# Attention scores as plain float32 products in the two row halves of the array, in place of split q and k

## The chip, the cores and the metric

The kernel runs on one core of one Trainium2 chip. What counts is the device time of one execution in microseconds (us), the median of three runs. In the rows, PE is TensorE, PEld its weight loads, DVE VectorE, ACT ScalarE, POOL GpSimd and SP SyncE, which issues most of the DMAs.

## The reference

Three stages follow each other: banded attention, a dense layer pair with x - tanh(x), and a second pair with a softmax-weighted, normalised middle. All arrays are float32.

```python
scores = scale * np.matmul(q, k.transpose(0, 1, 3, 2))        # B=4, H=8, S=576, D=64
scores = np.where(masks[None], scores, -1e9)                   # heads 0-3: the last 32 keys;
attn = softmax(scores)                                         # heads 4-7: every 4th of the last 128
x = np.matmul(attn, v)                                         # -> 2304 tokens x 512
h = x @ w_in                                                   # 512 -> 2048
y = (h - np.tanh(h)) @ w_out                                   # 2048 -> 512
h = y @ w_in2                                                  # 512 -> 1024
solu = h * softmax(h)
ln = (solu - mean(solu)) / np.sqrt(var(solu) + 1e-6) * g_ln
out = ln @ w_out2                                              # 1024 -> 512
```

## The kernel before, in words

The 2304 tokens are six groups of 384. The attention of a group is eight **units**; there are 48. A unit has two heads (h) and two blocks of 96 queries (b), each block with 128 keys, so four score tiles of 96 x 128. A unit goes through these pieces:

- its q and k are loaded (`load_qk`) as one tile `qkr`, with the 64 numbers of a head along the rows; its v is loaded by `load_v`;
- scores: units 0 to 19 (`NFU = 20`) in `qk_f32`, four plain float32 products on rows 0 to 63, into one PSUM bank. Units 20 to 47 in two halves (`qk_half`): `prep_unit` has rounded q and k to the short float32 format (`float32r`) and taken the remainder, the rows 64 to 127 hold a second copy of the data, and one product with 128 rows and 256 columns per score tile gives both parts of the sum; VectorE adds them and the mask;
- the four mask-and-minimum instructions on VectorE (L204 or L231), four exponentials on ScalarE (`sm_exp`), the division on GpSimd (`sm_norm`);
- the four transposes of the probabilities (`tr_pe`, tile `tp`), copied by ScalarE to `pt` (L260);
- `pv_pe`, for two units at a time: the eight products with v, whose outputs lie in rows 0 to 63 for one head and 64 to 127 for the other; ScalarE and VectorE take them out of PSUM (L284, L286).

The first eight units are computed at the start, with VectorE and ScalarE also decoding and splitting the first weights (L98 to L134). After that the dense layers run: `mm1(s)` is twelve products of 128 x 128 by 384 (L348) and `mm2(s)` the same (L375). The work of the other 40 units is threaded in between by hand. **A slot is one mm1 or one mm2**; slot 2s has mm1(s), slot 2s+1 has mm2(s-5). `plan` gives each piece its slot: the scores of unit u stand in slot p, its transposes and pv in later ones.

```python
p = 4 * u - 41 if u >= 2 * NU else (2, 6, 8, 12, 14, 16, 18, 20)[u - u0]
q = p + 2 if u >= 2 * NU or u < u0 + 4 else p + 1
...
if u0 <= u - 1 < u1:
    piece(q, lambda u=u: tr_pe(u - 1, a_ps, "at"))
if u % 4 == 1 and u0 <= u - 5 < u1:
    for w in (u - 5, u - 3):
        piece(q + 1, lambda w=w: pv_pe(w, a_ps, "at"))
```

The TensorE part of a piece comes behind the slot's mm1 or mm2. What takes it out of PSUM is queued on ScalarE or VectorE only in the next slot, behind that slot's weight decoding and tanh. All pieces take their PSUM banks in turn from one pool of two, `a_ps`; in the start-up they come from `st_ps`, with two banks each for scores, transposes and pv. Each engine works its instructions in the order written.

Of the kernel before, what the change touches and what calls it, by code (L numbers as in the profile page):

```python
# [7 lines left out]
F32 = mybir.dt.float32  # L8
# [16 lines left out]
NQ, NK = 96, 128  # L25
NU = 8
QC, KC = 4 * NQ, 4 * NK
KD = DM // 128
NF = FF // 128
NF2 = FF2 // 128  # L30
# [10 lines left out]
def tile_kernel(ctx: ExitStack, tc: tile.TileContext, qk, vw, cst, w_in, w_out, w_in2, w_out2, g_ln, out):  # L41
# [4 lines left out]
    wi_p = ctx.enter_context(tc.tile_pool(name="wi", bufs=1, side="left"))  # L46
    wo_p = tc.alloc_tile_pool(name="wo", bufs=1, side="left")
    cv_p = tc.alloc_tile_pool(name="cv", bufs=2, side="left")
    ys_p = qs_p = None
    g_p = ctx.enter_context(tc.tile_pool(name="g", bufs=2, side="right"))  # L50
    x_p = ctx.enter_context(tc.tile_pool(name="x", bufs=2, side="right"))
    at_p = tc.alloc_tile_pool(name="at", bufs=2, side="right")
# [8 lines left out]
    def mask_of(u, j):  # L61

        g, r = divmod(u, NU)
        hp, bp = divmod(r, 2)
        if hp < 2:
            return 0 if (4 * g + 2 * bp + j) % 6 == 0 else 1
        return (0, 2, 1)[g % 3]
# [80 lines left out]


    xt, un = {}, {}  # L150
    NFU = 20

    def load_qk(u):

        if u < NU:
            r = wo_p.tile([128, 1024], F32, tag=f"wo{NU + u}", name=f"qkr{u}")[:, 0:QC + KC]
        else:
            r = at_p.tile([128, QC + KC], F32, tag="qkr", name=f"qkr{u}")
        n = 64 if u < NFU else 128
        nc.sync.dma_start(out=r[:n], in_=qk[u, :n])  # L160
        un[u] = dict(r=r)

    def load_v(u):
# [6 lines left out]
            load_qk(u)  # L170
            load_v(u)

    def prep_unit(u):
        if not NFU <= u < NU * NG:
            return []
        r = un[u]["r"]
        s = qs_p.tile([128, QC + 2 * KC], F32R, tag="qks", name=f"qks{u}")
        un[u]["s"] = s
        return [
            lambda: nc.scalar.copy(out=s[:, 0:QC + KC], in_=r),  # L180
            lambda: nc.vector.tensor_tensor(out=s[64:128, 0:QC], in0=r[64:128, 0:QC],
                                            in1=s[64:128, 0:QC].bitcast(F32), op=ALU.subtract),
            lambda: nc.vector.tensor_tensor(out=s[:, QC + KC:], in0=r[:, QC:],
                                            in1=s[:, QC:QC + KC].bitcast(F32), op=ALU.subtract),
        ]

    def new_p(u):
        d = un[u]
        d["p"] = at_p.tile([NQ, 4, NK], F32, tag="p", name=f"p{u}", bufs=3)
        for t in ("nm", "sm", "rs"):  # L190
            d[t] = at_p.tile([NQ, 4], F32, tag=t, name=f"{t}{u}")

    def qk_f32(u, pool, tag):

        d = un[u]
        new_p(u)
        ps = pool.tile([128, 512], F32, tag=tag, name=f"qkp{u}")[:NQ, 0:KC].rearrange("p (b k) -> p b k", b=4)
        for b in range(4):
            nc.tensor.matmul(ps[:, b], d["r"][:64, b * NQ:(b + 1) * NQ],  # L199
                             d["r"][:64, QC + b * NK:QC + (b + 1) * NK], start=True, stop=True)  # L200

        def then():
            for b in range(4):
                nc.vector.tensor_tensor_reduce(  # L204
                    out=d["p"][:, b], in0=ps[:, b], in1=masks[:, mask_of(u, b % 2)], op0=ALU.add, op1=ALU.min,
                    scale=-0.125, scalar=3.0e38, accum_out=d["nm"][:, b:b + 1])
        return then

    def qk_half(u, hf, pool, tag):

        d = un[u]
        if hf == 0:
            new_p(u)
        ps = pool.tile([128, 512], F32, tag=tag, name=f"qkp{u}_{hf}")[:NQ, 0:4 * NK].rearrange(
            "p (b c k) -> p b c k", b=2, c=2)
        s = d["s"]
        for j in range(2):
            b = 2 * hf + j
            nc.tensor.matmul(  # L219
                ps[:, j], s[:, b * NQ:(b + 1) * NQ],  # L220
                s[:, QC:].rearrange("p (c k) -> p c k", c=2)[:, :, b * NK:(b + 1) * NK],
                start=True, stop=True)

        def then():
            m0, m1 = mask_of(u, 0), mask_of(u, 1)
            m = masks[:, 0:2] if m0 != m1 else masks[:, m0:m0 + 1].to_broadcast([NQ, 2, NK])
            p2 = d["p"][:, 2 * hf:2 * hf + 2]
            nc.vector.tensor_tensor(out=p2, in0=ps[:, :, 0], in1=m, op=ALU.add)
            for j in range(2):
                b = 2 * hf + j  # L230
                nc.vector.tensor_tensor_reduce(  # L231
                    out=d["p"][:, b], in0=ps[:, j, 1], in1=d["p"][:, b], op0=ALU.add, op1=ALU.min,
                    scale=-0.125, scalar=3.0e38, accum_out=d["nm"][:, b:b + 1])
        return then

    def sm_exp(u, bs=range(4)):
        d = un[u]
        for b in bs:
            nc.scalar.activation(out=d["p"][:, b], in_=d["p"][:, b], func=AF.Exp, scale=-1.0,  # L239
                                 bias=d["nm"][:, b:b + 1], accum_out=d["sm"][:, b:b + 1])  # L240

# [46 lines left out]


    st_ps = tc.alloc_tile_pool(name="st_ps", bufs=2, space=PSUM, side="left")  # L290
    load_qk(0)
    w_load()
    nc.sync.dma_start(out=cst_sb, in_=cst)
# [5 lines left out]
            w_load()  # L299
    back = None  # L300
    for r in range(NU + 3):
        t = qk_f32(r, st_ps, "qk") if r < NU else None
        b1 = pv_pe(r - 4, st_ps, "pv") if r % 2 == 0 and 0 <= r - 4 < NU else None
        b2 = tr_pe(r - 2, st_ps, "tr") if 0 <= r - 2 < NU else None
        if t:
            t()
        if back:
            back("h")
        if t:
            sm_exp(r)  # L310
        if 0 <= r - 1 < NU:
            sm_norm(r - 1)
        if back:
            back("l")
        back = b1
        if b2:
            b2()
        if r in SW:
            w_step(dve=True)
        if r in (4, 5):  # L320
            load_v(r + 2)
        if r in (6, 8):
            load_unit(NU + r // 2 - 3)
    back()
    nc.sync.dma_start(out=gl_sb, in_=g_ln)
    st_ps.release()

# [8 lines left out]
    def at(slot, fn):  # L338
        later.setdefault(slot, []).append(fn)
# [44 lines left out]
            nc.scalar.dma_start(out=y_dr[:, :, g * G:(g + 1) * G], in_=ys)  # L384

    u0, u1 = NU, NU * NG
    preps = []

    def piece(slot, fn):
        todo.setdefault(slot, []).append(fn)  # L390

    def plan():


        ready = 0
        for u in range(u0, u1 + 2):
            p = 4 * u - 41 if u >= 2 * NU else (2, 6, 8, 12, 14, 16, 18, 20)[u - u0]
            q = p + 2 if u >= 2 * NU or u < u0 + 4 else p + 1
            if u < u1:
                at(p + 1, lambda u=u: preps.extend(prep_unit(u + 1)))  # L400
                for i in (1, 1, 2):
                    at(p + i, lambda: preps.pop(0)() if preps else None)
                if u < NFU:
                    piece(p, lambda u=u: qk_f32(u, a_ps, "at"))
                    at(p + 1, lambda u=u: sm_exp(u))
                    at(p + 2, lambda u=u: sm_norm(u))
                else:
                    piece(p, lambda u=u: qk_half(u, 0, a_ps, "at"))
                    at(p + 2, lambda u=u: sm_exp(u, (0, 1)))
                    piece(p + 1, lambda u=u: qk_half(u, 1, a_ps, "at"))  # L410
                    at(p + 3, lambda u=u: sm_exp(u, (2, 3)))
                    at(p + 4, lambda u=u: sm_norm(u))
                at(p + 1, lambda u=u: load_unit(u + 2))
            if u0 <= u - 1 < u1:
                piece(q, lambda u=u: tr_pe(u - 1, a_ps, "at"))
# [3 lines that stand above are left out]
# [31 lines left out]
    for s in range(NS + LAG):  # L450
        if s == NS - NF:
            assert not todo and not later and not (wq or wld or wa or wf or wh), (todo, later)
            a_ps.release()
            at_p.release()
            qs_p.release()
            cv_p = tc.alloc_tile_pool(name="cv2", bufs=2, side="left", reuse_waits="tile")
            new_tops()
            h2a = tc.alloc_tile_pool(name="h2a", bufs=1, space=PSUM, side="right", reuse_waits="tile")
            p2 = tc.alloc_tile_pool(name="p2", bufs=2, side="right", reuse_waits="tile")
            wq.extend(wq2)  # L460
            w_load()
            w_load()
        for half in range(2):
            if ys_p is None and not (wq or wld or wa or wf or wh):
                cv_p.release()
                ys_p = tc.alloc_tile_pool(name="ys", bufs=1, side="left", reuse_waits="tile")
                qs_p = tc.alloc_tile_pool(name="qs", bufs=2, side="left", reuse_waits="tile")
            if half == 0:
                cur = mm1(s) if s < NS else None
            elif s >= LAG:  # L470
# [151 lines left out]
def _layout(q, k, v, moe_w_in, moe_w_out, moe2_w_in, moe2_w_out, moe2_g_ln):  # L622
    import numpy as np

    def blocks(a, n, back):
# [7 lines left out]
        for g in range(NG):  # L633
            for r in range(NU):
                hp, bp = divmod(r, 2)
                for h in range(2):
                    for b in range(2):
# [3 lines left out]
                        else:  # L641
# [3 lines left out]
        return o.reshape(NG * NU, 2, 2, n, D)  # L645

    qb, kb, vb = blocks(q, NQ, 0), blocks(k, NK, WIN), blocks(v, NK, WIN)
    qkt = np.concatenate([qb.transpose(0, 4, 1, 2, 3).reshape(NG * NU, D, QC),
                          kb.transpose(0, 4, 1, 2, 3).reshape(NG * NU, D, KC)], axis=2)
    qkt = np.concatenate([qkt, qkt], axis=1)  # L650
    vt = vb.transpose(0, 3, 2, 1, 4).reshape(NG * NU, NK, 4 * D)

    def bits(w):
# [38 lines left out]
```

## Time and profile before

| | us |
|---|---|
| median of three runs (727.55 to 729.39) | 728.31 |
| span of the profiled execution | 726.3 |
| TensorE busy in it | 708.8 |
| VectorE busy | 440.5 |
| ScalarE busy | 386.9 |
| GpSimd busy | 114.4 |

Of the profiled execution only the span is given, with no device time of its own; it is 2.0 us below the median of the runs. Busy times are sums of instructions, and TensorE's are pipelined, so that a busy TensorE still leaves open how fast it goes. The stages lie in time as follows: units 0 to 7 until about 37 us, mm1 and mm2 with units 8 to 19 until about 134 us, with units 20 to 47 until about 404 us, then the rest of the dense layers.

### The profile page before, as it was taken

The page shows a single profiled execution, that of the slowest core. Times are in us where ns is not written, and L with a number is a line of the kernel's source. Part 1 is how long each engine was busy: PE and PEld are TensorE (multiplying, and loading weights), DVE is VectorE, ACT ScalarE, POOL GpSimd, SP SyncE. Part 2 cuts the span into 40 slices and gives each one's busy share as a digit, 9 for nine tenths or more (in the row PEclk, how much of TensorE's full clock was granted, in tenths as well). Part 3 has the DMA queues.
Part 4 walks back from the last instruction along what each step waited for, and adds up shares of the span by engine and source line. Part 5 has one row for each costly group of instructions (what it writes and reads, how often), then busy time and mean ns, then how long its engine had stood idle before and what let it go on. Part 6 is the DMA issues. An engine that isn't in the chain of part 4 may idle for free.

```text
span 726.3 us, 11583 instructions
## 1 busy us (share of the span) xinstructions
PE 708.8 (98%) x4160; PEld 650.7 (90%) x4160; DVE 440.5 (61%) x1169; ACT 386.9 (53%) x1010; POOL 114.4 (16%) x190
## 2 busy tenths in 40 slices
PE   6888999999999999999999999999999999999997
PEld 5678999999999999999999999999888888888885
DVE  5987676476676667766666435554555454555452
ACT  5778776465555555555555334543354444444444
POOL 2212311011010111111110100101133221323110
PEclk9999999999999999999999999999999999999999
DMA  9985621132223211322230015543001110110001
GB/s 274 341 263 177 189 78 55 65 110 66 66 66 109 66 60 44 107 66 66 66 109 1 1 49 170 175 142 132 1 15 59 44 58 16 59 44 30 15 29 44
DMA packets 30313, 64.05 MB, mean 88 GB/s; under 512 B 2992, under 2 KB 16816, under 8 KB 30256
## 3 DMA queue, kind: packets, MB, share of 16 engines
q1 hardware_dynamic: 27088, 58.59, 25.4%
q10 hardware_dynamic: 3168, 4.72, 1.8%
q8 instruction: 33, 0.54, 0.3%
q14 instruction: 24, 0.20, 0.1%
HBM read 53.86 MB, written 9.44 MB: 87 GB/s over the span
## 4 chain that ended last, share of the span: by engine, by line
PE 92%; DVE 4%; DMA 1%; issue 1%; ACT 1%; POOL 0%; SPq 0%; ACTq 0%; POOLq 0%
PE y L375 28%; PE h L348 26%; PE po L585 14%; PE h L523 14%; PE zt L566 2%; PE pv L275 2%; PE tp L254 2%; PE qkp L219 2%; PE qkp L199 2%; DMA qkr<-in_qk_dram 1%; DVE p L204 1%; DVE wy_wi L123 1%; DVE wi L98 1%; DVE wi L134 0%; POOL p L247 0%
## 5 line engine op out<-in xcount | busy, mean ns | idle before, releaser
L348 PE MATMUL h<-x,wi 128*128 128x384 f32 x1152 | 220.0, 340 | 1.6 <-DVE t L359 1.6
L375 PE MATMUL y<-gs,wo 128*128 128x384 f32 x1152 | 217.4, 339 | 0.0
L375 PEld LDWEIGHTS y<-gs,wo 128*128 128x128 f32 x1152 | 199.8, 189 | 1.8
L348 PEld LDWEIGHTS h<-x,wi 128*128 128x128 f32 x1152 | 197.4, 189 | 3.2 <-DVE t L359 2.1
L247 POOL TENSOR_TENSOR p<-p,rs 96x512 f32<-96x512 f32 x47 | 57.2, 1217 | 350.4 <-DVE rs L245 323.5
L365 DVE TENSOR_TENSOR gs<-t,gs 128x384 fp32r<-128x384 f32 x96 | 77.4, 806 | 52.7 <-ACT gs L362 52.6
L523 PE MATMUL h<-w2i,yt 128*128 128x512 f32 x432 | 104.9, 397 | 0.0
L585 PE MATMUL po<-w2o,z 128*128 128x512 f32 x432 | 104.1, 396 | 0.1
L574 ACT ACTIVATE z<-zt,gl_sb 128x128 fp32r<-128x128 f32 x144 | 50.9, 366 | 96.6 <-PE zt L566 48.5
L585 PEld LDWEIGHTS po<-w2o,z 128*128 128x128 f32 x432 | 80.7, 188 | 20.4 <-ACT z L574 1.9
L523 PEld LDWEIGHTS h<-w2i,yt 128*128 128x128 f32 x432 | 79.7, 187 | 18.4
L359 DVE TENSOR_TENSOR t<-h,t 128x384 f32<-128x384 f32 x96 | 53.0, 552 | 69.8 <-ACT t L356 69.7
L575 DVE SCALAR_TENSOR_TENSOR z<-zt,gl_sb,z 128x128 fp32r<-128x128 f32 x144 | 48.9, 350 | 68.9 <-ACT z L574 68.9
L356 ACT ACTIVATE t<-h 128x384 f32<-128x384 f32 x96 | 46.8, 487 | 79.4 <-PE h L348 76.4
L239 ACT ACTIVATE p<-p,nm 96x128 f32<-96x128 f32 x192 | 74.9, 392 | 21.4 <-DVE nm L204 20.8
L362 ACT CAST gs<-t 128x384 fp32r<-128x384 f32 x96 | 48.8, 508 | 46.8 <-DVE t L359 46.8
L540 DVE SCALAR_TENSOR_TENSOR u<-h,e 128x1024 f32<-128x1024 f32 x18 | 22.0, 1224 | 24.1 <-ACT e L539 24.1
L199 PE MATMUL qkp<-qkr 64*96 64x128 f32 x160 | 29.4, 339 | 7.3 <-DMA qkr<-in_qk_dram 5.4
L441 POOL TENSOR_TENSOR yt<-yr,yt 128x1024 fp32r<-128x1024 f32 x9 | 22.8, 2538 | 86.8 <-DVE yt L440 86.8
L239 ACT ACTIVATION_READ_ACCUMULATOR p<-p,nm 96x1 f32 x192 | 36.1, 188 | 0.0
L199 PEld LDWEIGHTS qkp<-qkr 64*96 64x96 f32 x160 | 24.1, 205 | 11.8 <-DMA qkr<-in_qk_dram 5.7
L286 DVE TENSOR_TENSOR x<-pv,x 128x384 fp32r<-128x384 f32 x24 | 16.3, 699 | 25.1 <-ACT x L284 24.6
(64 smaller groups left out, 657.6 us busy)
## 6 DMA issues: line engine op xcount, KB each, us to landing
qkr<-in_qk_dram SPq DMA_DIRECT2D x28, 448.0 KB, 3.4
raw_wi<-in_w_in_dram SPq DMA_DIRECT2D x16, 511.8 KB, 7.2
raw_wo<-in_w_out_dram SPq DMA_DIRECT2D x16, 511.8 KB, 6.7
v<-in_vw_dram SPq DMA_DIRECT2D x48, 128.0 KB, 3.3
y_dr<-ys ACTq DMA_DIRECT2D x6, 768.0 KB, 3.9
yr<-y_dr SPq DMA_DIRECT2D x9, 512.0 KB, 4.2
out_dram<-o SPq DMA_DIRECT2D x18, 256.0 KB, 2.0
qkr<-in_qk_dram SPq DMA_DIRECT2D x20, 224.0 KB, 4.8
```

Source lines behind the costliest of these rows:

```text
L199: nc.tensor.matmul(ps[:, b], d["r"][:64, b * NQ:(b + 1) * NQ], d["r"][:64, QC + b * NK:QC + (b + 1) * NK], start=True, stop=True)
L239: nc.scalar.activation(out=d["p"][:, b], in_=d["p"][:, b], func=AF.Exp, scale=-1.0, bias=d["nm"][:, b:b + 1], accum_out=d["sm"][:, b:b + 1])
L247: eng.tensor_tensor(out=d["p"], in0=d["p"], in1=d["rs"].unsqueeze(2).to_broadcast([NQ, 4, NK]), op=ALU.mult)
L348: nc.tensor.matmul(ps, w[:, a, k * 128:(k + 1) * 128], xt[g, k][:, b], start=(n == 0), stop=(n == 3 * KD - 1))
L359: nc.vector.tensor_tensor(out=t, in0=ps, in1=t, op=ALU.subtract)
L362: nc.scalar.copy(out=gs[:, 0], in_=t)
L365: nc.vector.tensor_tensor(out=gs[:, 1], in0=t, in1=gs[:, 0].bitcast(F32), op=ALU.subtract)
L375: nc.tensor.matmul(yb[g][m], wo[c][:, a, m * 128:(m + 1) * 128], gs[:, b], start=(c == 0 and i == 0), stop=(c == NF - 1 and i == 2))
L523: nc.tensor.matmul(ps[:, n * 512:(n + 1) * 512], y[:, a, k, o:o + TT], w2i[2 * k + n][:, b], start=(q == 0), stop=(q == 3 * KD - 1))
L574: nc.scalar.activation(out=z[:, 0, c], in_=pp[n][:, j], func=AF.Copy, scale=gc)
L575: nc.vector.scalar_tensor_tensor(out=z[:, 1, c], in0=pp[n][:, j], scalar=gc, in1=z[:, 0, c].bitcast(F32), op0=ALU.mult, op1=ALU.subtract)
L585: nc.tensor.matmul(po, z[:, a, j], w2o[j][:, b], start=(q == 0), stop=(q == 3 * NF2 - 1))
```

## The change

All units get their scores from one function, `qk_pe`: four plain float32 products, head 0 on rows 0 to 63 and head 1 on rows 64 to 127, taken in turn, each head into a PSUM bank of its own. `prep_unit`, `qk_half` and the pool of the split operands are gone. A unit's load has 128 rows of 448 numbers, 224 KB, and the tile of it has three buffers. In the start-up the scores have a pool of four banks of their own (`sq_ps`). In `plan` the units from 20 on stand like those before: scores in slot p, exponentials in p+1, division in p+2 (before: p and p+1, p+2 and p+3, p+4).

```diff
+HQ, HK = 2 * NQ, 2 * NK
...
-            r = at_p.tile([128, QC + KC], F32, tag="qkr", name=f"qkr{u}")
-        n = 64 if u < NFU else 128
-        nc.sync.dma_start(out=r[:n], in_=qk[u, :n])
+            r = at_p.tile([128, HQ + HK], F32, tag="qkr", name=f"qkr{u}", bufs=3)
+        nc.sync.dma_start(out=r, in_=qk[u])
...
-    def prep_unit(u):
...
-    def qk_f32(u, pool, tag):
+    def qk_pe(u, pool, tag):
 
         d = un[u]
         new_p(u)
-        ps = pool.tile([128, 512], F32, tag=tag, name=f"qkp{u}")[:NQ, 0:KC].rearrange("p (b k) -> p b k", b=4)
-        for b in range(4):
-            nc.tensor.matmul(ps[:, b], d["r"][:64, b * NQ:(b + 1) * NQ],
-                             d["r"][:64, QC + b * NK:QC + (b + 1) * NK], start=True, stop=True)
+        ps = [pool.tile([128, 512], F32, tag=tag, name=f"qkp{u}_{h}")[:NQ, 0:HK].rearrange("p (b k) -> p b k", b=2)
+              for h in range(2)]
+        for b in range(2):
+            for h in range(2):
+                r = d["r"][64 * h:64 * h + 64]
+                nc.tensor.matmul(ps[h][:, b], r[:, b * NQ:(b + 1) * NQ], r[:, HQ + b * NK:HQ + (b + 1) * NK],
+                                 start=True, stop=True)
 
         def then():
-            for b in range(4):
-                nc.vector.tensor_tensor_reduce(
-                    out=d["p"][:, b], in0=ps[:, b], in1=masks[:, mask_of(u, b % 2)], op0=ALU.add, op1=ALU.min,
-                    scale=-0.125, scalar=3.0e38, accum_out=d["nm"][:, b:b + 1])
+            for b in range(2):
+                for h in range(2):
+                    j = 2 * h + b
+                    nc.vector.tensor_tensor_reduce(
+                        out=d["p"][:, j], in0=ps[h][:, b], in1=masks[:, mask_of(u, b)], op0=ALU.add, op1=ALU.min,
+                        scale=-0.125, scalar=3.0e38, accum_out=d["nm"][:, j:j + 1])
         return then
 
-    def qk_half(u, hf, pool, tag):
...
-    def sm_exp(u, bs=range(4)):
+    def sm_exp(u):
         d = un[u]
-        for b in bs:
+        for b in (0, 2, 1, 3):
...
+    sq_ps = tc.alloc_tile_pool(name="sq_ps", bufs=4, space=PSUM, side="right")
...
-        t = qk_f32(r, st_ps, "qk") if r < NU else None
+        t = qk_pe(r, sq_ps, "qk") if r < NU else None
...
-                at(p + 1, lambda u=u: preps.extend(prep_unit(u + 1)))
-                for i in (1, 1, 2):
-                    at(p + i, lambda: preps.pop(0)() if preps else None)
-                if u < NFU:
-                    piece(p, lambda u=u: qk_f32(u, a_ps, "at"))
-                    at(p + 1, lambda u=u: sm_exp(u))
-                    at(p + 2, lambda u=u: sm_norm(u))
-                else:
-                    piece(p, lambda u=u: qk_half(u, 0, a_ps, "at"))
-                    at(p + 2, lambda u=u: sm_exp(u, (0, 1)))
-                    piece(p + 1, lambda u=u: qk_half(u, 1, a_ps, "at"))
-                    at(p + 3, lambda u=u: sm_exp(u, (2, 3)))
-                    at(p + 4, lambda u=u: sm_norm(u))
+                piece(p, lambda u=u: qk_pe(u, a_ps, "at"))
+                at(p + 1, lambda u=u: sm_exp(u))
+                at(p + 2, lambda u=u: sm_norm(u))
                 at(p + 1, lambda u=u: load_unit(u + 2))
```

## Rows read from the trace of the kernel before

**Rows 1.** Busy time by stage: stretch, its length, each engine's busy us, clock, DMA.

```profile
10.00:39.00 29.00, 26.11 (x148) 21.29 (x149) 28.65 (x99) 23.15 (x78) 8.77 (x7) 1.00 1.05 331
...
136.00:404.00 268.00, 268.00 (x1792) 263.65 (x1791) 180.90 (x522) 145.34 (x409) 29.17 (x28) 1.00 0.22 70
```

**Rows 2.** Timeline of TensorE, a split unit: start, us, what, count.

```profile
149.49 0.40 PE L219 MATMUL qkp<-qks 128*96 128x256 f32 x2
149.73 2.24 PE L348 MATMUL h<-x,wi 128*128 128x384 f32 x12
151.81 0.40 PE L219 MATMUL qkp<-qks 128*96 128x256 f32 x2
```

**Rows 3.** Timeline of TensorE, two pv pieces and a plain float32 unit.

```profile
116.80 1.54 PE L275 MATMUL pv<-pt,v 128*64 128x96 f32 x32
...
128.32 2.25 PE L375 MATMUL y<-gs,wo 128*128 128x384 f32 x12
130.49 1.11 PE L199 MATMUL qkp<-qkr 64*96 64x128 f32 x8
131.53 2.36 PE L348 MATMUL h<-x,wi 128*128 128x384 f32 x12
133.73 2.24 PE L375 MATMUL y<-gs,wo 128*128 128x384 f32 x12
```

**Rows 4.** TensorE by line, 100 to 136 us: busy us, mean ns of one.

```profile
L199 PE MATMUL qkp<-qkr 64*96 64x128 f32 x26 | 3.7, 278 | 0.0
...
L275 PE MATMUL pv<-pt,v 128*64 128x96 f32 x32 | 1.5, 249 | 0.0
```

**Rows 5.** Timelines of TensorE and VectorE at the start, with idle time and releaser.

```profile
7.40 2.02 PE L199 MATMUL qkp<-qkr 64*96 64x128 f32 x8 [1.08 <-DMA qkr<-in_qk_dram]
...
9.46 0.29 DVE L204 CUSTOM_DVE_ANT_0 p<-qkp,cst_sb 96x128 f32<-96x128 f32 x1 [2.16 <-PE qkp L199]
```

**Rows 6.** Timelines of TensorE and ScalarE around unit 10.

```profile
54.24 1.11 PE L199 MATMUL qkp<-qkr 64*96 64x128 f32 x8 [0.49 <-DVE nm L204]
55.28 2.36 PE L348 MATMUL h<-x,wi 128*128 128x384 f32 x12
59.86 0.90 PE L254 MATMUL tp<-cst_sb,p 96*128 96x96 f32 x4 [2.22 <-POOL p L247]
60.47 3.57 PE L375 MATMUL y<-gs,wo 128*128 128x384 f32 x12
...
58.28 0.46 ACT L260 COPY pt<-tp 128x384 f32<-128x384 f32 x1
```

**Rows 7.** Timelines around units 12 and 14: TensorE, ScalarE, VectorE.

```profile
71.79 1.11 PE L199 MATMUL qkp<-qkr 64*96 64x128 f32 x8
...
85.38 1.11 PE L199 MATMUL qkp<-qkr 64*96 64x128 f32 x8 [0.51 <-DVE x L286]
...
72.25 0.45 ACT L260 COPY pt<-tp 128x384 f32<-128x384 f32 x1
...
84.77 1.22 DVE L286 TENSOR_TENSOR x<-pv,x 128x384 fp32r<-128x384 f32 x2 [0.40 <-ACT x L284]
```

**Rows 8.** Timeline of a later pv and the unit behind it.

```profile
158.10 1.22 DVE L286 TENSOR_TENSOR x<-pv,x 128x384 fp32r<-128x384 f32 x2 [2.04 <-ACT x L284]
...
160.33 0.40 PE L219 MATMUL qkp<-qks 128*96 128x256 f32 x2
```

**Rows 9.** Instructions by line, whole span: busy us, mean ns | idle before, releaser.

```profile
L180 ACT CAST qks<-qkr 128x896 fp32r<-128x896 f32 x28 | 26.3, 938 | 0.0
...
L228 DVE TENSOR_TENSOR p<-qkp,cst_sb 96x256 f32<-96x256 f32 x56 | 23.3, 415 | 2.9 <-PE qkp L219 0.7
...
L183 DVE TENSOR_TENSOR qks<-qkr,qks 128x512 fp32r<-128x512 f32 x28 | 19.0, 678 | 0.0
...
L181 DVE TENSOR_TENSOR qks<-qkr,qks 64x384 fp32r<-64x384 f32 x28 | 15.6, 556 | 0.9
```

**Rows 10.** DMA issues, whole span: count, KB each, median us to landing.

```profile
qkr<-in_qk_dram SPq DMA_DIRECT2D x28, 448.0 KB, 3.4
```

More of the change, by code (lines that the diff above doesn't have):

```diff
@@ L48, in tile_kernel @@
     cv_p = tc.alloc_tile_pool(name="cv", bufs=2, side="left")
-    ys_p = qs_p = None
+    ys_p = None
     g_p = ctx.enter_context(tc.tile_pool(name="g", bufs=2, side="right"))
@@ L150, in tile_kernel @@
     xt, un = {}, {}
-    NFU = 20
     def load_qk(u):
         if u < NU:
-            r = wo_p.tile([128, 1024], F32, tag=f"wo{NU + u}", name=f"qkr{u}")[:, 0:QC + KC]
+            r = wo_p.tile([128, 1024], F32, tag=f"wo{NU + u}", name=f"qkr{u}")[:, 0:HQ + HK]
         else:
-            r = at_p.tile([128, QC + KC], F32, tag="qkr", name=f"qkr{u}")
-        n = 64 if u < NFU else 128
-        nc.sync.dma_start(out=r[:n], in_=qk[u, :n])
+            r = at_p.tile([128, HQ + HK], F32, tag="qkr", name=f"qkr{u}", bufs=3)
+        nc.sync.dma_start(out=r, in_=qk[u])
         un[u] = dict(r=r)
@@ L171, in load_unit @@
             load_v(u)
-    def prep_unit(u):
[L174 to L185, printed above, removed]
     def new_p(u):
@@ L207, in qk_f32 @@
         return then
-    def qk_half(u, hf, pool, tag):
+    def sm_exp(u):
         d = un[u]
[L212 to L234, printed above, removed]
@@ L236, in sm_exp @@
-    def sm_exp(u, bs=range(4)):
-        d = un[u]
-        for b in bs:
+        for b in (0, 2, 1, 3):
             nc.scalar.activation(out=d["p"][:, b], in_=d["p"][:, b], func=AF.Exp, scale=-1.0,
@@ L326, in tile_kernel @@
     st_ps.release()
+    sq_ps.release()
     h_ps = tc.alloc_tile_pool(name="h_ps", bufs=2, space=PSUM, side="left", reuse_waits="tile")
@@ L386, in tile_kernel @@
     u0, u1 = NU, NU * NG
-    preps = []
     def piece(slot, fn):
@@ L454, in tile_kernel @@
             at_p.release()
-            qs_p.release()
             cv_p = tc.alloc_tile_pool(name="cv2", bufs=2, side="left", reuse_waits="tile")
@@ L466, in tile_kernel @@
                 ys_p = tc.alloc_tile_pool(name="ys", bufs=1, side="left", reuse_waits="tile")
-                qs_p = tc.alloc_tile_pool(name="qs", bufs=2, side="left", reuse_waits="tile")
             if half == 0:
@@ L647, in _layout @@
     qb, kb, vb = blocks(q, NQ, 0), blocks(k, NK, WIN), blocks(v, NK, WIN)
-    qkt = np.concatenate([qb.transpose(0, 4, 1, 2, 3).reshape(NG * NU, D, QC),
-                          kb.transpose(0, 4, 1, 2, 3).reshape(NG * NU, D, KC)], axis=2)
-    qkt = np.concatenate([qkt, qkt], axis=1)
+    qkt = np.concatenate([qb.transpose(0, 1, 4, 2, 3).reshape(NG * NU, 128, HQ),
+                          kb.transpose(0, 1, 4, 2, 3).reshape(NG * NU, 128, HK)], axis=2)
     vt = vb.transpose(0, 3, 2, 1, 4).reshape(NG * NU, NK, 4 * D)
```

## The prediction, made before the changed kernel was run

> **What bounds the kernel now.** I read the busy time by stage first. Between 136 and 404 us TensorE is busy for all 268.00 us, while VectorE and ScalarE have a third or more to spare [rows 1]. The list of waits has no entry for TensorE in that stretch. So there a microsecond of TensorE time costs a microsecond, and time taken from VectorE or ScalarE is worth nothing. In the start-up (10 to 39 us) VectorE is the full engine, 28.65 of 29.00 us [rows 1]. The timeline then tells what each kind of piece costs TensorE. Only distances between starts count: matmuls overlap, so the printed durations are too long to be added.
>
> **The split scores (units 20 to 47) that go.** A half unit starts at 149.49 and the next group at 149.73, so it costs 0.24 us; the group of twelve behind it takes 151.81 - 149.73 = 2.08 [rows 2]. Two halves: 0.48 us a unit, with no loss at the borders.
>
> **The plain float32 unit, as units 8 to 19 have it.** From the group at 128.32 to the group at 133.73 are 5.41 us; two plain groups are 4.16, so the unit between them costs 1.25 us [rows 3]. Its eight matmul records (two for each product) span 1.11 us, one lasts 0.28 [rows 3, 4], so they start (1.11 - 0.28) / 7 = 0.12 us apart, 0.84 us from the first to the end of the row; the remaining 0.4 us lie at the two borders, where products of 128 rows meet products of 64.
>
> **What the two halves can give.** The trace of before has no product in the lower row half. It has column halves: the pv products alternate between output rows 0 to 63 and 64 to 127. Their 32 records span 1.54 us, one lasts 0.25, so they start 0.042 us apart, with 96 moving columns each [rows 3, 4]: 0.43 ns a column, where the scores, with 128 columns and 0.12 us, take 0.94. So alternating column halves run two at a time, at full gain, in float32. The new loop alternates the halves in the same order (b outside, h inside). If row halves do the same, 0.42 us (each of seven gaps halved) to 0.48 us (four of seven gaps gone) leave the 1.25, and I take a unit at 0.81 us. The bounds are 0.77 and 1.25 (no overlap); a unit's border cost stays, since products of 64 rows are still entered and left.
>
> The Trainium skill, "TensorE: Matmul & The Clock Gate", Part 3 (Packing small matmuls), says that tiles in different row groups run concurrently, and gives 3.07 times for four row tiles, three quarters of the full gain. By that figure two would give about 1.5 times, an estimate: the products would fall from 0.84 to 0.56 us, the unit to about 0.97, and the sum below would end near 742. The pv records speak for the full gain, but for columns.
>
> **The sum for the long stretch.** Units 20 to 47: 28 x (0.81 - 0.48) = +9.2 us. Units 8 to 19: the first three (up to the one at 54.24 us, [rows 6]) lie where TensorE waits for others anyway, so nine count: 9 x (0.81 - 1.25) = -4.0 us.
>
> **What leaves ScalarE and VectorE.** Per unit of the split kind a cast of 0.94 us on ScalarE, two subtractions (0.56 and 0.68) and two adds of the mask (0.42 each) on VectorE [rows 9]. All of it lies beside a TensorE that is never idle [rows 1]: worth 0. The loads of units 20 to 47, 448 KB each [rows 10], become 224 KB, asked for two units ahead: also 0. The softmax of these units comes one or two slots earlier on ScalarE, VectorE and GpSimd, and its transposes two slots after the scores as before; nobody waits for it on TensorE in that stretch: 0.
>
> **Start-up.** At 9.46 us VectorE had waited 2.16 us for the second unit's products, which started when their load came at 7.40 and took 2.02 us [rows 5]. The pace there is half that of later (2.02 against 1.11 us for the same eight), though the clock column reads 1.00 here too [rows 1]. Overlapped they end some 0.9 us sooner, and from there to about 39 us VectorE hardly pauses [rows 1]; so the 0.9 us carry through: -0.9 (bounds 0 and -2). The loads of these units have the same bytes in 128 rows instead of 64, so twice as many shorter packets, while the DMA share is full [rows 1]; I take 0, and if they land later, the 0.9 goes, hence the bound of 0. The later units of the start-up gain nothing: VectorE covers them.
>
> **The new waits.** The pool of the long stretch has two banks. A unit took one and takes both. Where another piece stands in the same slot just ahead of the unit, the unit's second half needs the bank which that piece has just filled, and the copy that empties it is only in the next slot's ScalarE or VectorE work. Everything behind on TensorE waits too, as it goes in order. By the slot list this happens three times.
> - Unit 10 (slot 8, behind the transposes of unit 8). Its products started at 54.24; the copy of those transposes ran at 58.28 to 58.74, as ScalarE was behind [rows 6]. So the second half starts at 58.8 and the next group of twelve, which ran at 55.28, starts at 59.5. It ends at 61.7, or 2 us later if it pays the slow pace that the group at 60.47 paid before (3.57 us against the 2.24 of a later one [rows 3]). Before, the transposes behind it waited until 59.86 for GpSimd [rows 6]; so the loss is some 1.8 us without a change of clock loss, 2.0 with the half-microsecond by which the scores of unit 10 come later. I take +2.0; bounds 0.3 (no slow group any more) and 3.9 (one of double length).
> - Unit 12 (slot 14): products at 71.79, copy until 72.70 [rows 7]: +0.7, as a quarter of the unit is done before.
> - Unit 14 (slot 18): it waited 0.51 us for the first of two VectorE evacuations, and must now wait for the second, until 84.77 + 1.22 = 85.99 instead of 85.38 [rows 7]: +0.6.
>
> The Trainium skill, "TensorEngine Tiling (Array Packing)", Gotcha 1 (PSUM Pressure), says the same against this change: row tiles must write different banks. No run of before shows what a shared bank would do.
>
> In later slots pv and the unit behind it are a whole group apart: the evacuations are over at 158.10 + 1.22 = 159.32, and the unit came at 160.33 [rows 8]. So nothing there; if that microsecond of cover went, it would cost about ten times what it lacks.
>
> Sum: +9.2 - 4.0 - 0.9 + 2.0 + 0.7 + 0.6 = +7.6 us on the span of 726.3. The profile gives no other time for its execution than that span; the runs' median of 728.3 lies 2.0 above it, which I leave as it is: 728.3 + 7.6 = **735.9 us**.
>
> **Rivals.** Let c be the cost of a unit. The time moves by 28 (c - 0.48) + 9 (c - 1.25) + 2.4 us (the waits less the start-up).
> - Full overlap, c = 0.77 to 0.85, with the bounds of the waits and the start-up: 731 to 740. Chance 0.57.
> - Part of it. A product's two records, in turn on their half, hold up the other half: five steps in place of eight, 3 x 0.12 saved, c = 0.89. Or the two weight loads, 96 columns each against the 64 of pv [rows 4], take turns, and half of the saving goes: c = 1.02. By the formula +10.6 to +15.5, 739 to 744. For it: no row halves at once are in the trace. Against: the pv records, two of which start together all the way. Chance 0.2.
> - No overlap, so the change does not do what it says: c = 1.25, 28 x 0.77 + 3.3 = +24.9, 753. Chance 0.12.
> - The other side: the border cost of 0.4 us is not paid. If the array goes from row halves to all rows as cheaply as it did around the split units, c is about 0.44, and the formula gives -1.1 - 7.3 + 2.4 = -6, 722. It decides below c = 0.60, where the formula gives zero. Against it: the plain unit pays it in every one of its places in the trace, and the new unit is entered and left in the same way. Chance 0.07; another 0.04 for c close to 0.60.
>
> **From these to the numbers.** A difference of 0.3% (2.2 us) is about what can be told from none. Faster has the border rival, 0.07; same 0.04 and a little of the low end of the forecast, 0.05; slower the rest, 0.88. The range of 8 in 10 leaves out no overlap and the faster side (0.19 together) and takes in the part overlap: 731 to 745.
>
> **What would show it.** In the profile after: a unit's eight score records spanning about 0.65 us instead of 1.11; 5.41 us between the groups around a unit down to about 4.97; TensorE still without idle time from 136 us on; a wait of the score products on the ScalarE copy of tp near 54 to 59 us and smaller ones near 72 and 86 us; VectorE's and ScalarE's busy time down by about 58 and 26 us (the sums of [rows 9]) with no gain from it. The prediction is wrong if a unit's eight records still span 1.1 us (then 753), if the borders vanish (then near 722), or if the waits on the two banks recur in every unit beyond 100 us.

## The result and the profile after

The changed kernel takes 737.2 us against 728.4 for the kernel before, medians of four runs each; the ratio is 1.0118, 95% interval 1.010 to 1.0137. So it is slower by 8.8 us. The forecast was 735.9, in a range of 731 to 745. The spans of the two profiled executions are 736.0 and 726.3, 9.7 apart, and the accounts below are made between these. Two executions of the runs below lie far from all others of their kernels and are left out of every figure: one of 871.6 us in the run with split late units, at a granted clock of 0.76, and one of 2476 us in the run with zeros, in which the groups of twelve took some 7.5 us.

The timeline of TensorE around one plain unit, in the columns of [rows 3]:

```profile
129.05 2.25 PE L340 MATMUL y<-gs,wo 128*128 128x384 f32 x12
131.22 0.68 PE L187 MATMUL qkp<-qkr 64*96 64x128 f32 x8
131.83 2.35 PE L313 MATMUL h<-x,wi 128*128 128x384 f32 x12
134.02 2.24 PE L340 MATMUL y<-gs,wo 128*128 128x384 f32 x12
```

From 129.05 to 134.02 are 4.97 us, less two groups of 2.08: a unit costs 0.81 us, as forecast (before, 1.25 plain and 0.48 split [rows 2, 3]). The eight records span 0.68 us instead of 1.11.

The busy time by stage, in the columns of [rows 1]:

```profile
10.00:39.00 29.00, 22.15 (x150) 16.60 (x151) 28.65 (x95) 22.93 (x76) 8.77 (x7) 1.00 1.04 396
...
136.00:404.00 268.00, 268.00 (x1845) 253.86 (x1844) 124.60 (x400) 122.74 (x373) 27.92 (x28) 1.00 0.15 47
```

VectorE is relieved of 56 us between 136 and 404 us (180.90 before) and ScalarE of 23 (145.34). TensorE is full for all 268.00 us as before, so nothing came of it. In the start-up TensorE has 4 us less to do, and VectorE is as full as it was.

The start, in the columns of [rows 5]:

```profile
7.84 1.17 PE L187 MATMUL qkp<-qkr 64*96 64x128 f32 x8 [3.27 <-DMA qkr<-in_qk_dram]
...
9.04 0.29 DVE L194 CUSTOM_DVE_ANT_0 p<-qkp,cst_sb 96x128 f32<-96x128 f32 x1 [1.49 <-PE qkp L187]
```

The second unit's products take 0.85 us less, but they start 0.44 us later, when their load lands. VectorE begins 0.42 us earlier.

Around unit 10, TensorE and ScalarE, to be read beside [rows 6]:

```profile
37.17 6.07 PE L313 MATMUL h<-x,wi 128*128 128x384 f32 x24
...
50.67 3.92 PE L313 MATMUL h<-x,wi 128*128 128x384 f32 x12 [1.77 <-DVE t L324]
...
54.85 0.46 PE L187 MATMUL qkp<-qkr 64*96 64x128 f32 x2
58.41 1.16 PE L187 MATMUL qkp<-qkr 64*96 64x128 f32 x6 [3.10 <-ACT pt L223]
59.50 4.21 PE L313 MATMUL h<-x,wi 128*128 128x384 f32 x12
63.50 0.84 PE L217 MATMUL tp<-cst_sb,p 96*128 96x96 f32 x4
64.05 2.60 PE L340 MATMUL y<-gs,wo 128*128 128x384 f32 x12
66.49 2.25 PE L313 MATMUL h<-x,wi 128*128 128x384 f32 x12
68.66 0.68 PE L187 MATMUL qkp<-qkr 64*96 64x128 f32 x8
...
57.88 0.47 ACT L223 COPY pt<-tp 128x384 f32<-128x384 f32 x1
```

The same in the trace of before, where the first two groups, mm1(6) and unit 11 stand as follows:

```profile
37.58 5.20 PE L348 MATMUL h<-x,wi 128*128 128x384 f32 x24
...
63.88 2.24 PE L348 MATMUL h<-x,wi 128*128 128x384 f32 x12
66.05 1.11 PE L199 MATMUL qkp<-qkr 64*96 64x128 f32 x8
```

This is the wait that was forecast. The first product of unit 10 (two records) runs at 54.85; the other three wait 3.10 us, until ScalarE's copy of the transposes at 57.88 to 58.35 has emptied the bank. The group behind takes 4.21 us and not 2.25, and the one at 50.67 takes 3.92.

The granted clock by stretches of 4 us (last three numbers of a line: clock, DMA share, GB/s):

```profile
48.00:52.00 4.00, 2.23 (x15) 1.80 (x14) 3.26 (x8) 2.98 (x7) 1.91 (x1) 0.87 0.78 257
52.00:56.00 4.00, 3.31 (x15) 2.88 (x13) 3.46 (x13) 3.44 (x13) 0.00 (x0) 0.70 0.70 261
56.00:60.00 4.00, 1.59 (x8) 1.32 (x9) 2.68 (x10) 2.83 (x9) 1.91 (x1) 0.73 0.00 0
60.00:64.00 4.00, 4.00 (x16) 3.90 (x15) 2.78 (x10) 2.97 (x11) 1.34 (x1) 0.50 0.72 218
64.00:68.00 4.00, 4.00 (x24) 4.00 (x23) 2.32 (x4) 2.34 (x5) 0.56 (x1) 0.92 0.36 136
```

Before, the clock was below 1.00 in two of these stretches:

```profile
56.00:60.00 4.00, 1.78 (x11) 1.46 (x10) 3.08 (x14) 3.59 (x11) 1.91 (x1) 0.97 0.95 256
60.00:64.00 4.00, 4.00 (x17) 4.00 (x18) 2.95 (x8) 3.75 (x11) 1.75 (x1) 0.60 0.43 169
```

A clock of 0.50 is the lower level, 1.2 GHz, for the whole stretch. The shortfalls add up to 4 x (0.13 + 0.30 + 0.27 + 0.50 + 0.08) = 5.1 us of full-speed time, 10.2 us at the lower level; before, to 1.7 and 3.4 us. Much of it lies where TensorE waits anyway (from 56 to 60 us it is busy for 1.59 of 4.00), so these figures are not yet a loss.

Units 12 and 14, beside [rows 7]:

```profile
73.97 0.46 PE L187 MATMUL qkp<-qkr 64*96 64x128 f32 x2
74.94 0.67 PE L187 MATMUL qkp<-qkr 64*96 64x128 f32 x6 [0.52 <-ACT pt L223]
...
87.66 0.46 PE L187 MATMUL qkp<-qkr 64*96 64x128 f32 x2 [0.51 <-DVE x L249]
88.32 0.67 PE L187 MATMUL qkp<-qkr 64*96 64x128 f32 x6 [0.20 <-DVE x L249]
```

Both waits for the second bank are there. Beyond 100 us none follows.

### The profile page after: what moved, and what is told of

It reads as the page before. It is cut to its first block, busy times and chain, and to the rows that moved or that the text cites. A ratio compares the mean times of both kernels' runs of the same rounds, so it can differ in the third digit from the quotient of the medians.

```text
span 736.0 us, 11625 instructions
## 1 busy us (share of the span) xinstructions
PE 711.4 (97%) x4272; PEld 642.1 (87%) x4272; DVE 388.0 (53%) x1057; ACT 367.1 (50%) x982; POOL 114.3 (16%) x190
## 4 chain that ended last, share of the span: by engine, by line
PE 91%; DMA 3%; DVE 2%; ACT 1%; issue 1%; SPq 0%; ACTq 0%
PE y L340 28%; PE h L313 27%; PE po L536 14%; PE h L474 14%; PE qkp L187 3%; PE zt L517 2%; PE pv L238 2%; PE tp L217 2%; DMA raw_wi<-in_w_in_dram 2%; DMA qkr<-in_qk_dram 2%; ACT top L112 0%; DVE p L194 0%; DVE wy_wi L124 0%; DVE wy_wo L124 0%; DVE wi L99 0%
## 5 line engine op out<-in xcount | busy, mean ns | idle before, releaser
L313 PE MATMUL h<-x,wi 128*128 128x384 f32 x1152 | 227.1, 347 | 1.8 <-DVE t L324 1.8
L313 PEld LDWEIGHTS h<-x,wi 128*128 128x128 f32 x1152 | 201.3, 192 | 7.4 <-DVE t L324 2.0
L330 DVE TENSOR_TENSOR gs<-t,gs 128x384 fp32r<-128x384 f32 x96 | 79.2, 825 | 67.7 <-ACT gs L327 67.4
L194 DVE CUSTOM_DVE_ANT_0 p<-qkp,cst_sb 96x128 f32<-96x128 f32 x192 | 44.1, 282 | 22.1 <-PE qkp L187 15.2
L187 PE MATMUL qkp<-qkr 64*96 64x128 f32 x384 | 38.4, 317 | 12.2 <-DMA qkr<-in_qk_dram 6.7
L187 PEld LDWEIGHTS qkp<-qkr 64*96 64x96 f32 x384 | 26.3, 179 | 24.2 <-issue 8.2
```

The costliest lines, as they stand in the source:

```text
L187: nc.tensor.matmul(ps[h][:, b], r[:, b * NQ:(b + 1) * NQ], r[:, HQ + b * NK:HQ + (b + 1) * NK], start=True, stop=True)
L313: nc.tensor.matmul(ps, w[:, a, k * 128:(k + 1) * 128], xt[g, k][:, b], start=(n == 0), stop=(n == 3 * KD - 1))
L330: nc.vector.tensor_tensor(out=gs[:, 1], in0=t, in1=gs[:, 0].bitcast(F32), op=ALU.subtract)
```

## The experiments

The question was which part of the loss belongs to the 28 late units and which to the waits at the start, and what a unit's 0.81 us consist of.

**Split scores again for units 20 to 47.** In the kernel before, units 0 to 19 get `qk_pe` and the four start-up banks; the rest stays.

```diff
-        n = 64 if u < NFU else 128
-        nc.sync.dma_start(out=r[:n], in_=qk[u, :n])
+        n = HQ + HK if u < NFU else QC + KC
+        nc.sync.dma_start(out=r[:, 0:n], in_=qk[u, :, 0:n])
...
-                    piece(p, lambda u=u: qk_f32(u, a_ps, "at"))
+                    piece(p, lambda u=u: qk_pe(u, a_ps, "at"))
```

> Row halves for units 0 to 19, split scores as before for units 20 to 47. Theory (each of the 28 late units costs 0.33 us more in row halves): the 9.3 us between units 20 and 47 go, the result is that of the changed kernel less 9.3, about 728.0, no different from before by more than 1. Rival (the loss sits in the early waits and the slow stretch of the clock, and the late units come out even): it stays within 2 us of 737.

Measured: 726.8 us, ratio to before 0.9992 (0.9982 to 1.0001). Against the changed kernel's 1.0118 that is 1.26% of 728 us, 9.2 us. So the late units cost what the count of 28 x 0.33 says, and without them the change is worth nothing measurable: the nine early units' gain and the waits cancel.

**All units plain, in one row half.** The kernel before with `NFU = 48`.

```diff
-    NFU = 20
+    NFU = 48
```

> The kernel before with all 48 units as plain float32 products on rows 0 to 63 and in one bank, so no split and no row halves. Theory (overlap of the row halves saves 0.44 of 1.25 us a unit): 28 x (1.25 - 0.48) = 21.6 above before, about 750. Rival (a unit costs what it costs through its borders, the overlap gives little): near the changed kernel, 737 to 741.

Measured: 749.5 us, ratio 1.0299 (1.0279 to 1.0318). The timeline of TensorE around a late unit:

```profile
304.20 2.25 PE L375 MATMUL y<-gs,wo 128*128 128x384 f32 x12
306.38 1.11 PE L199 MATMUL qkp<-qkr 64*96 64x128 f32 x8
...
309.61 2.25 PE L375 MATMUL y<-gs,wo 128*128 128x384 f32 x12
```

309.61 - 304.20 - 4.16 = 1.25 us a unit. The two row halves at once are thus worth 0.44 us a unit; they make plain scores cheaper, but not as cheap as the split ones.

**One half after the other.** The changed kernel with its two loops exchanged.

```diff
-        for b in range(2):
-            for h in range(2):
+        for h in range(2):
+            for b in range(2):
```

> The changed kernel with the loops over head and block exchanged: both products of one row half, then both of the other. Theory (overlap needs neighbours in the queue on different halves): only the products at the change of half overlap, a unit takes 0.81 + 2 x 0.11 = 1.0 to 1.2 us, 37 units: 744 to 751. Rival (each half has a queue of its own and works it off independently): eight records still span 0.68 us, the time stays at 737.

Measured: 737.3 us, ratio 1.0132 (1.0119 to 1.0145). The rival was right: the order does not matter. The timeline of TensorE at unit 12, where the second half waits for its bank, and at a unit without a wait:

```profile
73.44 0.67 PE L187 MATMUL qkp<-qkr 64*96 64x128 f32 x4
74.42 0.68 PE L187 MATMUL qkp<-qkr 64*96 64x128 f32 x4 [0.30 <-ACT pt L223]
...
130.72 0.69 PE L187 MATMUL qkp<-qkr 64*96 64x128 f32 x8
```

At unit 12 the four records of one half run by themselves and span 0.67 us, then those of the other, 0.68. Where nothing waits, all eight span 0.69 us, although the four of one half stand ahead of the four of the other in the program. So the two halves run side by side from the first record to the last.

**Own banks for unit 10.** In the changed kernel it takes two of the four banks of the y pool, idle before mm2(0); `qk_pe` accepts a tag for each half.

```diff
-                piece(p, lambda u=u: qk_pe(u, a_ps, "at"))
+                piece(p, lambda u=u: qk_pe(u, y_ps, ("y2", "y3")) if u == 10 else qk_pe(u, a_ps, "at"))
```

> The changed kernel, unit 10 alone takes its two banks from the y pool, which is not used before mm2(0). Theory (the wait for the copy of the transposes of unit 8 costs 3.1 us and a second slow stretch of the clock behind it): no idle time of 3.1 us before the products of unit 10, mm2(0) starts at 60 to 61 instead of 64.05, the time falls by 3 to 4 us to about 733.7. Rival (ScalarE and VectorE set the pace until 60 us, the wait is only where TensorE would wait anyway): the time falls by less than 1 us.

Measured: 734.3 us, ratio 1.0089 (1.0074 to 1.0104), 0.29% or 2.1 us below the changed kernel by the ratios and 2.9 by the medians: a little short of the 3 to 4 that the theory asked for, and beyond the rival's 1. The two intervals just touch (1.010 and 1.0104), so the traces decide. The timeline of TensorE at the first groups and from unit 10 on:

```profile
37.50 5.78 PE L313 MATMUL h<-x,wi 128*128 128x384 f32 x24
...
54.48 0.68 PE L187 MATMUL qkp<-qkr 64*96 64x128 f32 x8
55.09 2.36 PE L313 MATMUL h<-x,wi 128*128 128x384 f32 x12
59.76 0.55 PE L217 MATMUL tp<-cst_sb,p 96*128 96x96 f32 x4 [2.31 <-POOL p L210]
60.09 3.46 PE L340 MATMUL y<-gs,wo 128*128 128x384 f32 x12
63.35 2.73 PE L313 MATMUL h<-x,wi 128*128 128x384 f32 x12
66.01 0.68 PE L187 MATMUL qkp<-qkr 64*96 64x128 f32 x8
```

The wait has gone and mm2(0) starts at 60.09 instead of 64.05. It is slow, as in the kernel before, and the group behind it in part. From mm1(0) to the scores of unit 11 this run takes 66.01 - 37.50 = 28.51 us, the changed kernel 31.49 and the kernel before 28.47. So the edit takes away the whole of the term, 3.0 us.

**Both edits at once.** Split scores for units 20 to 47, own banks for unit 10.

> Both earlier edits at once: row halves for units 0 to 19 with own banks for unit 10, split scores for units 20 to 47. Theory (the 9.3 us of the late units and the 3 us of the wait are separate terms): 728.0 - 0.6 - 2.9, about 724.4, faster than before by 0.4 to 0.6%. Rival (without the wait the time is lost elsewhere in the same stretch, as VectorE and ScalarE set its pace): within 1 us of the run with split late units, 727.

Measured: 724.1 us, ratio 0.9940 (0.9927 to 0.9952). It lies 2.7 us below the run with split late units by the medians and 3.8 by the ratios, where the same edit took 2.9 and 2.1 from the changed kernel. So the terms add, to within some 2 us, and the rival falls. This version is faster than both kernels.

**Every score product of units 20 to 47 twice.** The changed kernel; the second product overwrites the first with the same values.

```diff
-        for b in range(2):
+        for b in (0, 1, 0, 1) if u >= 20 else (0, 1):
```

> The changed kernel, units 20 to 47 issue each of their score products twice (16 records a unit instead of 8, same results). Theory (of a unit's 0.81 us the overlapped products are 0.43 and the borders, paid once a unit, 0.37): 28 x 0.43 = +12.0, about 749. Rival (the cost goes by products, with no fixed part): 28 x 0.81 = +22.7, about 760.

Measured: 748.8 us, ratio 1.0275 (1.0259 to 1.0290). The timeline of TensorE around a late unit:

```profile
303.85 2.25 PE L340 MATMUL y<-gs,wo 128*128 128x384 f32 x12
306.02 1.12 PE L187 MATMUL qkp<-qkr 64*96 64x128 f32 x16
...
309.27 2.24 PE L340 MATMUL y<-gs,wo 128*128 128x384 f32 x12
```

A unit with 16 records costs 5.42 - 4.16 = 1.26 us, 0.45 more than with eight. So 0.45 us belong to the eight records and 0.36 to the borders.

**All 128 rows, with zeros.** The changed kernel, q with zeros in the rows of the other head, so that each product has 128 rows and still gives one head's scores.

```diff
-                r = d["r"][64 * h:64 * h + 64]
-                nc.tensor.matmul(ps[h][:, b], r[:, b * NQ:(b + 1) * NQ], r[:, HQ + b * NK:HQ + (b + 1) * NK],
+                r, j = d["r"], 2 * h + b
+                nc.tensor.matmul(ps[h][:, b], r[:, j * NQ:(j + 1) * NQ], r[:, QC + b * NK:QC + (b + 1) * NK],
                                  start=True, stop=True)
```

> The changed kernel without row halves: q has zeros in the rows of the other head, so each plain float32 product uses all 128 rows and stands between the dense products without a change of rows; banks and order as in the changed kernel, loads of 320 KB. Theory (the 0.37 us at the borders come from the change between 128 and 64 rows): eight records at 0.109 us and no border, 0.87 to 0.92 us a unit against 0.81, 37 units: +2 to +4, 739 to 741. Rival (the border belongs to plain float32 products as such): 1.24 us a unit, +16, about 753.

Measured: 740.4 us, ratio 1.0160 (1.0145 to 1.0176).

> The kernel with zeros in q and all 128 rows once more, for its trace. Theory: the eight records of a unit span 1.04 us or less, no extra time at the borders, about 0.90 us from group to group for the unit (5.06 between the groups around one). Rival: a border of 0.3 to 0.4 us is there as well, and the time of the earlier run (740.4) came about otherwise.

Measured, in one execution: 740.2 us. The timeline of TensorE around a late unit:

```profile
308.31 2.24 PE L340 MATMUL y<-gs,wo 128*128 128x384 f32 x12
310.39 1.03 PE L187 MATMUL qkp<-qkr 128*96 128x128 f32 x8
...
313.34 2.25 PE L340 MATMUL y<-gs,wo 128*128 128x384 f32 x12
```

313.34 - 308.31 - 4.16 = 0.87 us a unit, which is eight records at 0.109 and nothing else: with all 128 rows there is no border cost. The same eight records on 64 rows cost 1.25 us (one row half, above); the difference is 0.38 us. The row halves, at 0.81 us, are thus only 0.06 us a unit cheaper than rows filled up with zeros: what running side by side saves, 0.44 us, the borders nearly take back.

**TensorE busy while it waits.** The run with both edits, units 9 and 10 issue their products four times.

```diff
-        for b in range(2):
+        for b in (0, 1, 0, 1, 0, 1, 0, 1) if u in (9, 10) else (0, 1):
```

> As the run with split late units and own banks for unit 10, but units 9 and 10 issue their products four times (some 1.3 us more of TensorE each, in a stretch where TensorE waits for others). Theory (the slow stretch of the clock near 60 us follows from TensorE's idle time there): no slow stretch, the group mm2(0) takes 2.3 instead of 3.5 us, 1 to 1.7 us faster than without the extra products, about 723. Rival (the clock falls all the same): the same time or up to 1.3 us slower.

Measured: 723.2 us, ratio 0.9929 (0.9917 to 0.9941), 1.0 us below the run without the extra products; the two intervals overlap, so the traces decide. First the timeline of TensorE in the run without, then in the one with them: the wait ahead of mm2(0) and the groups behind:

```profile
58.15 0.55 PE L260 MATMUL tp<-cst_sb,p 96*128 96x96 f32 x4 [2.33 <-POOL p L253]
58.48 3.50 PE L383 MATMUL y<-gs,wo 128*128 128x384 f32 x12
61.78 2.67 PE L356 MATMUL h<-x,wi 128*128 128x384 f32 x12
```

```profile
57.66 0.55 PE L260 MATMUL tp<-cst_sb,p 96*128 96x96 f32 x4 [1.01 <-POOL p L253]
57.99 2.33 PE L383 MATMUL y<-gs,wo 128*128 128x384 f32 x12
60.16 2.25 PE L356 MATMUL h<-x,wi 128*128 128x384 f32 x12
```

Some 2.6 us of work that nobody needs were put where TensorE would have waited. The granted clock is then 1.00 all through (0.91 from 56 to 60 us and 0.66 from 60 to 64 without them), and the two groups take 1.6 us less (2.17 and 2.18 from start to start against 3.30 and 2.60). From mm1(0) to mm2(2) 1.2 us of it remain (34.23 us against 35.42), as the wait at unit 12 grows by 0.4. The rest of the difference between the spans (720.7 against 722.3) is the start-up, which was 0.4 us shorter in this execution. This is shown for this place only.

## Why the prediction was right, term by term

| term | forecast | measured | from |
|---|---|---|---|
| start-up | -0.9 | -0.4 | mm1(0) at 37.17; before 37.58 |
| wait of unit 10, with the clock | +2.0 | +3.0 | mm1(6) starts at 66.49; before at 63.88; less the -0.4 |
| nine early units | -4.0 | -4.0 | 0.81 against 1.25 us |
| unit 12 | +0.7 | +1.0 | transposes to mm2(2): 2.00 us; before 1.47; a free unit would have saved 0.44 |
| unit 14 | +0.6 | +0.7 | pv to mm2(4): 3.31; before 3.09; same |
| 28 late units | +9.2 | +9.4 | the span's 9.7 less the 0.3 at unit 19 (134.02 against 133.73 [rows 3]) |
| sum | +7.6 | +9.7 | |

**The price of a unit.** The step from column halves to row halves held: 0.81 us, and the rivals of partial or no overlap fall with the first timeline. The Trainium skill, "TensorE: Matmul & The Clock Gate", Part 3, would by its figure for four row tiles have made it 0.97, an estimate; here two halves give the full gain (0.68 us against 1.11 for eight records, of which the last one's own length of 0.28 is in both).

**The border.** The prediction kept 0.4 us at the borders and said what would follow if they went. They stayed, at 0.36 us, and the run with zeros shows them to come from the change between 128 and 64 rows. (The 0.12 us between two records took in a longer first gap; at 0.109 the eight are 0.87 of a plain unit's 1.25 us, and its borders 0.38.) The Trainium skill, "TensorEngine Tiling (Array Packing)", Key Properties, says that a change of the tiling mode drains TensorE. The runs agree that such a change costs time; that a drain is what takes it, they do not show. The border is why the changed kernel is slower: at 0.45 us for the records alone, a unit would be cheaper than the split one's 0.48.

**The waits on two banks.** Where and behind which copy they come was right in all three places. The size of the first was off: +3.0 in place of +2.0, inside the bounds of 0.3 to 3.9. The term that was too small is the clock behind the wait. Up to the wait nothing is lost: mm1(4) starts at 50.67 (before 51.06), and ScalarE comes to the copy at 57.88 (before 58.28 [rows 6]), both 0.4 us ahead as at the start. So neither the slower first two groups (6.07 us against 5.20) nor the low clock from 51 us on cost time; the run with own banks, the same up to there, had no such drop (the granted clock is 1.00 from 48 to 60 us), and why it comes in one trace and not in another was not tried. Behind the wait, the prediction counted one slow group as before: mm2(0) took 63.88 - 60.47 = 3.41 us, 1.2 above the 2.17 that it takes at full speed. In the changed kernel the group at 59.50 takes 4.00 us to the next start and mm2(0) 2.44, 1.8 and 0.3 above their full speed (2.19 and 2.17). That is 0.8 of the missing 1.0 us.

**The start-up.** The second unit's products started 0.44 us later in this execution, and half of the gain went. But three more traces have the same loads at the start, those of the exchanged loops, of own banks for unit 10 and of the doubled products: there these products start at 7.33, 8.18 and 7.45 us (before 7.40), and mm1(0) at 36.64, 37.50 and 36.76 (before 37.58). So the landing moves by 0.85 us between executions of the same code; where it comes as early as before, mm1(0) gains 0.8 to 0.9, as forecast. The -0.4 is what one execution had, and that shorter packets land later is not shown.

The forecast rested on the unit's price, and this came out to the hundredth: the saving of 0.44 us lies between the 0.42 and 0.48 that it was worked out from. The other 2.1 us between the sums are the clock behind the wait (1.0), a start-up that varies between executions (0.5) and small terms.

## What to carry to other kernels

Where a full engine sets the end, price each form of a piece by the distance between the groups around it, not by its own duration: that shows what switching costs as well, and here the switching made the cheaper-looking form the dearer one. A handful of products in row halves between full products pays the change each time. Many of them together would share it; by the figures here (0.36 us a visit, 0.45 for a unit's records against 0.48 split) it would take a dozen units in a row to match the split form, an estimate that no run tried. A pool that just suffices for one bank per piece can make TensorE wait as soon as a piece takes two: here in three places, each with another piece just ahead in the same slot. Look for such neighbours, and for idle banks elsewhere. That gave the version with units 0 to 19 in row halves, the rest split and unit 10 in the y pool, 724.1 us (723.2 with the needless products).

## What the runs showed of the hardware that was not expected

The two row halves work off their products independently of the order in which they are written: with one half's four records all ahead of the other's, the eight still span 0.69 us, where four alone span 0.67. That each engine works in the order written holds at a wait (at unit 12 of the changed kernel six records wait, although one product's bank is free), but not for the starts in the two halves. And a few microseconds of needless products in a waiting stretch of TensorE kept its clock at the upper level and were repaid (1.6 us in the two groups behind, of which 1.2 remained by mm2(2), and 1.0 us in the median, with intervals that overlap).
